# Fused attention and mixer: PSUM as one tile of eight banks, with one exponential and one normalising instruction for two heads

## The chip, the cores and the metric

The kernel runs on one core of one Trainium2 chip. The metric is the device time of one launch in microseconds. The kernel before was timed three times: median 333.76 us, from 333.57 to 334.19. One more execution was taken by the hardware profiler; its span, from the first to the last instruction on the core, is 330.8 us.

## The reference

Causal attention with 16 beacon keys in front, followed by a token mixer of rank 32 and a two-layer perceptron, both with a residual:

```python
B, H, S, Nb, D = 8, 8, 576, 16, 64          # batch, heads, tokens, beacons, head width
k_all = concat(beacon_k, k); v_all = concat(beacon_v, v)      # 592 keys
scores = q @ k_all^T / sqrt(D), causal behind the beacons
a = exp(scores - max); a /= a.sum() + 1e-9
x = (a @ v_all), heads side by side          # B x 576 x 512
h = x^T @ U @ V                              # U 576x32, V 32x576: over the tokens
u = x + h^T
out = u + relu(u @ w_ch1) @ w_ch2            # 512 -> 2048 -> 512
```

## The kernel before

**Work.** A pair is two heads of one batch; there are 32, four to a batch. The keys of a pair (592, in five chunks of 128) stand on the partitions, the queries along the free axis, so that the scores come out transposed and their exponentials can be the stationary operand of the next product. Scores go into PSUM banks (512 f32 words on each of 128 partitions) in four groups `g`, packed so that no masked block is computed: 496, 464, 496 and 208 columns a head. For each group and each head there is one bank `sps`, one exponential on ScalarE (ACT) into an SBUF tile `expt` of that head, and VectorE (DVE) zeroes the diagonal blocks with a minimum against a mask (`mask_head`, L349, one instruction a head). The weighting (`av_unit`, L424) multiplies a head's exponentials by its values with a column of ones beside them: 15 matmuls into one bank `po` of 5 x 65 words, whose 65th words are the sums. DVE takes their reciprocals (L436, 128x5) and multiplies (L437, 128x5x64) into the batch's `xb`.

`visit` inside `score_units` (L354) issues scores and exponentials of pairs 0 to 7, two groups at a time; `by_head` sets the order of its four exponentials (head 0's two first, or group by group). The outer `visit` (L396) does this for later pairs, with up to four units at a time, where a unit is one group of one pair or two short groups (208 and 208) in one bank.

The mixer of a batch (`mix_units`) ends in `most` (L486): four matmuls `ups` (L490), one for each 128 columns of the model, each on 32 rows of the array and into a bank of its own, drained on DVE by `settle` (L477). The perceptron takes 512 tokens at a time: first layer `gps` (L675) with a relu on ACT (L683) or DVE (L681), or by Strassen's seven products in `qpsA`, `qpsD`, `qpsF` (L701), which DVE adds to kept parts (L723) before a relu (L728); second layer in products `mpsA` to `mpsF` (L829, L909), which DVE adds to `kept` or `ob` tiles (L849). These steps wait in a list, `fill(n)` takes n of them.

**Order.** Every engine's order is written out by hand: the whole runs under a manual schedule, where each engine executes its instructions in the order in which Python issued them. `play` reads lines of short words (`e` scores, `a` and `b` head 0's and head 1's weighting, `m` masks, `f` one step of the list), and `long_slot` arranges the later pairs. A pair's two weightings are not neighbours: steps of the list are put between them.

**Banks.** There are eight PSUM banks. `pst` (L107) hands them out strictly in the order in which Python returned them by `emptying` (L114): first in, first out. It is called when the instructions are issued, so which bank a matmul writes is fixed in the program. The framework lets the first matmul into a bank wait for the last reader of what it held before. A bank is returned right behind its reader in program order, not when that reader has run.

```python
emptied = list(range(8))
...
b = emptied.pop(0)
t = psum.tile(shape, dtype, tag=f"bank{b}", name=name)
...
emptied.append(bank_of.pop(id(t))[0])
```

Of the kernel before, what the change touches and what calls it, by code (L numbers as in the profile page):

```python
# [18 lines left out]
P = 128  # L19
# [11 lines left out]
def kernel(  # L31
# [13 lines left out]
    nc = tc.nc  # L45
    B, H, S, D = q.shape
# [56 lines left out]

    emptied = list(range(8))
    bank_of = {}

    def pst(shape, dtype, name):  # L107

        b = emptied.pop(0)
        t = psum.tile(shape, dtype, tag=f"bank{b}", name=name)  # L110
        bank_of[id(t)] = (b, t)
        return t

    def emptying(t):  # L114
        emptied.append(bank_of.pop(id(t))[0])

# [29 lines left out]
    def clear_gaps(ex):  # L146
        for g in range(1, 4):
            nc.vector.memset(ex[:, AT[g] + gw[g] : AT[3] if g == 1 else blk[(3 if g == 3 else 4, 4)] + P], 0.0)

# [23 lines left out]
    NE = 4  # L173
    expts = [const.tile([P, EW], F16, name=f"expt{i}", tag=f"expt{i}") for i in range(NE)]
    flat = w2.rearrange("p (i a) c -> p i (a c)", i=NE)
    lent = [flat[:, i, 0:EW] for i in range(NE)]
    kTs = [const.tile([P, NH2, NC * P], F16, name=f"kT{i}", tag=f"kT{i}") for i in range(2)]
# [166 lines left out]
    def score_units(c, qT, kT, ex, early=False):  # L344

        def mask_head(i):
            e = ex[i][:, 0 : 3 * SLOT]
# [5 lines left out]
        def visit(gs, idle=0, by_head=True, between=None):  # L353
            turn = [(g, i) for i in range(2) for g in gs] if by_head else [(g, i) for g in gs for i in range(2)]  # L354
            ps = {(g, i): pst([P, 512], F32, name=f"sps{i}") for g, i in turn}
            keep_warm(ps[gs[0], 0], idle)
            if early:
                for g in gs:
                    for i in range(2):
                        for ch, qa, w, o in groups[g]:  # L360
                            if ch in (g, 4):
                                n = nq[ch]
                                nc.tensor.matmul(
                                    ps[g, i][:, ds(o, n)], identb, negmask[:, min(ch, 1), 0:n],
                                    start=ch == g, stop=False, skip_group_check=True,
                                )
            for g in gs:
                for ch, qa, w, o in groups[g]:
                    for i in range(2):
                        hp = slice(D * i, D * i + D)  # L370
                        nc.tensor.matmul(  # L371
                            ps[g, i][:, ds(o, w)], kT(hp, c, ch), qT[hp, c, ds(qa, w)],
                            start=not early, stop=True, skip_group_check=early,
                        )

            def exps(g, i):
                nc.scalar.activation(  # L377
                    out=ex[i][:, ds(AT[g], gw[g])], in_=ps[g, i][:, 0 : gw[g]], func=AF.Exp, scale=scale
                )

            for n, (g, i) in enumerate(turn):
                if between and n == len(gs):
                    between()
                exps(g, i)
                emptying(ps[g, i])

        def masks():
            for i in () if early else range(2):
                mask_head(i)

        return [
            lambda idle=0, between=None, gs=[0, 1]: visit(gs, idle, between=between),
            lambda gs=[2, 3], by_head=True: visit(gs, 0, by_head), masks, mask_head,
        ]

    def visit(parts):  # L396

        at = {p: (p % NH2, qTs[p // NH2], keys_of(p // NH2, kTs[p // NH2 % 2]), expts_of(p)) for p, _ in parts}
        both = {(p, g) for p, g in parts if g == 3 and (p + 1, 3) in parts}
        units = [[(p, g, 0), (p + 1, g, gw[g])] if (p, g) in both else [(p, g, 0)]  # L400
                 for p, g in parts if (p - 1, g) not in both]
        ps = {}
        for unit in units:
            banks = [pst([P, 512], F32, name=f"sps{i}") for i in range(2)]
            for p, g, at0 in unit:
                c, qT, kT, _ = at[p]
                for ch, qa, w, o in groups[g]:
                    for i in range(2):
                        hp = slice(D * i, D * i + D)
                        nc.tensor.matmul(  # L410
                            banks[i][:, ds(at0 + o, w)], kT(hp, c, ch), qT[hp, c, ds(qa, w)],
                            start=True, stop=True, skip_group_check=len(unit) > 1,
                        )
            ps[unit[0]] = banks
        for unit in units:
            for i in range(2):
                bank = ps[unit[0]][i]
                for p, g, at0 in unit:
                    nc.scalar.activation(  # L419
                        out=at[p][3][i][:, ds(AT[g], gw[g])], in_=bank[:, ds(at0, gw[g])], func=AF.Exp, scale=scale  # L420
                    )
                emptying(bank)

    def av_unit(b, h, ex, vs, xb):  # L424
        po = pst([P, NT, E], F32, name="po")
        for j in range(NT):
            for c in range(j + 1):
# [5 lines left out]
                    stop=(c == j),  # L433
                )
        r = rec[:, b * H + h, :, :]
        nc.vector.reciprocal(out=r, in_=po[:, :, D : D + 1])  # L436
        nc.vector.tensor_tensor(  # L437
            out=xb[:, :, ds(h * D, D)], in0=po[:, :, 0:D], in1=r.broadcast_to([P, NT, D]), op=ALU.mult
        )
        emptying(po)  # L440

    def x_into(xb, ups, cc, js, a, first):
# [778 lines left out]
    def expts_of(p):  # L1221
        return [(lent if p in (2, 3) else expts)[(2 * p + i) % NE] for i in range(2)]

# [7 lines left out]
    def av_of(p):  # L1231
        b, c = divmod(p, NH2)
        if c == 0:
            assert not coming or b < DT0
            xbs[b] = xbp.tile([P, NT, DM], F16, name="xb", tag="xb")
        return [
            lambda i=i: av_unit(b, 2 * c + i, expts_of(p)[i], vss[b % 2], xbs[b]) for i in range(2)
        ]
# [4 lines left out]
    avs = {}  # L1243
    ON_PE = (0, 1, 4)
    ACT_KEYS = (8, 10, 11, 12, 14, 15)

# [102 lines left out]
    with tc.manual_schedule(engines={ENG.PE, ENG.Activation, ENG.DVE, ENG.SP, ENG.Pool}):  # L1349
# [18 lines left out]
        cast = small_loads()  # L1368
        sc[1]([3, 2], False)
        sc = scores_of(1)  # L1370
# [26 lines left out]
        t2[1]()  # L1397
        sc[1]([3, 2], False)
        t2[0]()
        t3[1]()  # L1400
        later[0][0]()
        t3[0]()
        later[0][1]([3, 2], False)
        av[0]()
# [265 lines left out]
```

## Time and profile before

| | |
|---|---|
| time, median of 3 | 333.76 us (333.57 to 334.19) |
| span of the profiled execution | 330.8 us, at a mean granted TensorE clock of 0.998 |
| time that lies around the span, by the median | 3.0 us |
| TensorE (PE) | 323.5 us busy, 98% of the span, 3670 matmuls |
| VectorE (DVE) | 262.7 us, 79%, 606 instructions |
| ScalarE (ACT) | 196.6 us, 59%, 430 instructions |
| GpSimd (POOL) | 167.1 us, 51% |
| exponentials | L377 48 and L419 192 in the two costliest groups, 20.4 and 82.0 us |
| normalising | L436 64 times, 186 ns in the mean; L437 64 times, 491 ns |

In the rows of the trace a line shows the start in microseconds from the span's beginning, the busy time, engine, line and operation, output and inputs by the program's names, shapes, and the number of equal instructions in a row; in brackets stands the engine's idle time before, with what ended it. In rows that group instructions, the numbers behind the bar are the group's busy time, the mean of one in ns, and the idle time ahead of the group with its releasers. A row of stretches shows for each engine its busy time in that stretch with its number of instructions, in the order PE, weight loads, DVE, ACT, POOL, and then the granted clock, the DMA share and the rate. Spans of neighbouring instructions of one engine overlap a little, because an end includes the tail of writing.

### The profile page before, as it was taken

The numbers are of one execution on the slowest core, as the hardware profiler recorded it, in microseconds if no ns is written. First come the engines' busy times: TensorE is split into PE (matmuls) and PEld (weight loads), VectorE is DVE, ScalarE is ACT, GpSimd is POOL, SyncE is SP. The second block draws the span as 40 slices with busy tenths as digits, with TensorE's granted clock in tenths as the row PEclk, the third lists the DMA queues.
The fourth block names the chain that finished last, engine by engine and source line by source line (L and its number), as shares of the span: only waits on it lengthen the run. The fifth ranks groups of instructions, "written<-read, shape, count | busy, mean of one in ns | idle before, by whom it ended". The sixth has DMA issues, their size and how long they took to land.

```text
span 330.8 us, 9298 instructions
## 1 busy us (share of the span) xinstructions
PE 323.5 (98%) x3670; PEld 228.9 (69%) x3670; DVE 262.7 (79%) x606; ACT 196.6 (59%) x430; POOL 167.1 (51%) x263
## 2 busy tenths in 40 slices
PE   8899999999999999999999999999999999999994
PEld 3565555555578656876588888765787888788783
DVE  6675888668998668786878777877788898798993
ACT  5967962689972677348844695379636613713710
POOL 8897734568238960689048923950284036030030
PEclk9999999999999999999999999999999999999999
DMA  7999999999999996999999999995014512305004
GB/s 159 142 168 156 173 190 202 193 193 156 97 129 164 196 153 98 96 183 138 131 166 165 138 139 152 98 216 80 12 65 117 74 44 98 65 8 168 19 4 131
DMA packets 150562, 41.99 MB, mean 127 GB/s; under 512 B 131313, under 2 KB 149937, under 8 KB 150513
## 3 DMA queue, kind: packets, MB, share of 16 engines
q0 software_dynamic: 87568, 18.18, 73.2%
q1 hardware_dynamic: 62144, 22.41, 38.1%
q10 hardware_dynamic: 800, 0.75, 0.7%
q8 instruction: 30, 0.49, 0.7%
q14 instruction: 20, 0.16, 0.2%
HBM read 37.45 MB, written 9.44 MB: 142 GB/s over the span
## 4 chain that ended last, share of the span: by engine, by line
PE 94%; ACT 3%; DVE 1%; issue 0%
PE gps L675 21%; PE po L428 9%; PE mpsA L909 9%; PE qpsA L701 6%; PE mpsD L829 6%; PE sps L410 6%; PE cps L1053 4%; PE gps L1027 4%; PE mpsE L829 3%; PE mpsC L829 3%; PE mpsB L829 3%; PE qpsD L701 3%; ACT expt L377 2%; PE mpsF L829 2%; PE mpsD L909 2%; PE tps L299 2%
## 5 line engine op out<-in xcount | busy, mean ns | idle before, releaser
L577 POOL TENSOR_TENSOR ob<-ob,ut 128x128 f32<-128x128 f32 x104 | 50.0, 510 | 121.2 <-DVE ob L849 59.4
L419 ACT ACTIVATE expt<-sps 128x496 f16<-128x496 f32 (+2 forms) x192 | 82.0, 542 | 41.8 <-PE sps L410 41.8
L675 PE MATMUL gps<-uT,w 128*128 128x512 f16 (+1 forms) x368 | 78.1, 351 | 0.0
L829 PEld LDWEIGHTS <-gT 128*128 128x128 f16 x576 | 54.2, 98 | 8.8 <-issue 2.6
L675 PEld LDWEIGHTS <-w 128*128 128x128 f16 x368 | 33.2, 98 | 25.6 <-issue 1.3
L653 DVE TENSOR_TENSOR gT<-gT 128x1024 f16<-128x1024 f16 (+3 forms) x87 | 47.0, 561 | 0.9
L239 POOL DMA_DIRECT2D vs<-in_v_dram x50 | 40.0, 810 | 14.9 <-DMA w<-in_moe_w_ch_dram 11.2
L683 ACT ACTIVATE gT<-gps 128x512 f16<-128x512 f32 x63 | 37.5, 619 | 16.1 <-PE gps L675 11.9
L428 PEld LDWEIGHTS <-expt 128*128 128x128 f16 x900 | 33.9, 98 | 7.9 <-issue 1.5
L428 PE MATMUL po<-vs,expt 128*128 128x65 f16 x900 | 36.4, 194 | 0.2
L909 PEld LDWEIGHTS <-gT 128*128 128x128 f16 x336 | 31.2, 98 | 4.0
L437 DVE TENSOR_TENSOR xb<-po,rec 128x320 f16<-128x320 f32 x64 | 31.4, 491 | 2.2
L349 DVE TENSOR_TENSOR expt<-expt,bigmask 128x768 f16<-128x768 f16 x54 | 30.3, 600 | 0.4 <-ACT expt L419 0.2
L720 ACT ACTIVATE kept<-qpsA 128x512 f32<-128x512 f32 x18 | 10.9, 603 | 24.1 <-PE qpsA L701 13.2
L436 DVE RECIPROCAL rec<-po 128x5 f32<-128x5 f32 x64 | 11.9, 186 | 13.6 <-PE po L428 13.2
L410 PE MATMUL sps<-qT,kT 64*128 64x80 f16 (+4 forms) x288 | 22.6, 281 | 0.0
L377 ACT ACTIVATE expt<-sps 128x496 f16<-128x496 f32 (+2 forms) x48 | 20.4, 569 | 0.6 <-PE sps L371 0.6
L909 PE MATMUL mpsA<-w,gT 128*128 128x256 f16 x160 | 19.1, 273 | 0.0
L410 PEld LDWEIGHTS <-kT 64*128 64x128 f16 x288 | 10.2, 94 | 12.8 <-issue 8.3
L681 DVE TENSOR_SCALAR gT<-gps 128x512 f16<-128x512 f32 x17 | 11.7, 689 | 8.9 <-PE gps L675 8.7
L1126 POOL DMA_DIRECT2D st<-in_k_dram x20 | 16.9, 859 | 1.2 <-DVE pr L294 0.9
L1126 POOL DMA_DIRECT2D st<-in_q_dram x20 | 16.9, 872 | 0.7 <-DVE rec L436 0.7
(159 smaller groups left out, 541.4 us busy)
## 6 DMA issues: line engine op xcount, KB each, us to landing
out_dram<-ob SPq DMA_DIRECT2D x33, 256.0 KB, 3.5
vs<-in_v_dram POOLq DMA_DIRECT2D x18, 128.0 KB, 6.7
w<-in_moe_w_ch_dram POOLq DMA_DIRECT2D x4, 512.0 KB, 6.2
w<-in_moe_w_ch_dram POOLq DMA_DIRECT2D x2, 1024.0 KB, 12.7
st<-in_k_dram POOLq DMA_DIRECT2D x12, 128.0 KB, 6.6
st<-in_q_dram POOLq DMA_DIRECT2D x12, 128.0 KB, 8.6
st<-in_k_dram POOLq DMA_DIRECT2D x4, 288.0 KB, 12.0
st<-in_q_dram POOLq DMA_DIRECT2D x4, 288.0 KB, 12.6
```

Source lines behind the costliest of these rows:

```text
L239: nc.gpsimd.dma_start(out=dst[a : a + nq[j], j, :, :], in_=src[hs, ds(q0[j], nq[j]), :].rearrange("h p d -> p h d"))
L410: nc.tensor.matmul(banks[i][:, ds(at0 + o, w)], kT(hp, c, ch), qT[hp, c, ds(qa, w)], start=True, stop=True, skip_group_check=len(unit) > 1,)
L419: nc.scalar.activation(out=at[p][3][i][:, ds(AT[g], gw[g])], in_=bank[:, ds(at0, gw[g])], func=AF.Exp, scale=scale)
L428: nc.tensor.matmul(po[:, j, :], ex[0 : nk[c], ds(blk[(c, j)], P)], vs[0 : nk[c], ds(c * H * E + h * E, E)], start=(c == 0), stop=(c == j),)
L437: nc.vector.tensor_tensor(out=xb[:, :, ds(h * D, D)], in0=po[:, :, 0:D], in1=r.broadcast_to([P, NT, D]), op=ALU.mult)
L577: nc.gpsimd.tensor_tensor(out=o[:, i, ds(c, w)], in0=x[:, i, ds(c, w)], in1=y[:, i, ds(c, w)], op=op)
L653: nc.vector.tensor_tensor(out=o[:, ds(d0, n)], in0=x[:, ds(d0, n)], in1=y[:, ds(d0, n)], op=op)
L675: nc.tensor.matmul(g[:, ds(o, w)], w1[:, cc, ts(dc, P)], uT[:, cc, ds(at, w)], start=(cc == 0 and o == 0), stop=(cc == NCC - 1), skip_grou ...
L683: nc.scalar.activation(out=cell["g"][:, dc, :], in_=g, func=AF.Relu)
L829: nc.tensor.matmul(ps, a()[:, d, ds(P * i, P)], bm[:, d, ds(c0, w)], start=fresh and d == 0 and i == 0, stop=d == HF - 1, skip_group_check ...
L909: nc.tensor.matmul(ps, a()[:, d, ds(P * i, P)], bm[:, d, ds(c0, w)], start=fresh and d == 0, stop=d == HF - 1, skip_group_check=True,)
L1126: coming.append(lambda d=dst, s=src, a=m[j] - nq[j], n=m[j], j=j: nc.gpsimd.dma_start(out=d[a:n, j, :, :], in_=s[:, ds(q0[j], nq[j]), :].r ...
```

## The change

PSUM becomes one tile, `whole`, of eight banks. Four things follow in the code.

- **One exponential for both heads.** The scores of head 0 and head 1 of a group are put into neighbouring banks, the `expt` tiles hold both heads side by side, and one activation reads 2 x 496 (or 464, 208) words. ACT issues 32 instead of 64 exponentials at L377 and 96 instead of 192 at L419 in the program. The order of `by_head` falls away. The minimum with the mask stays one instruction a head.
- **One normalising for both heads.** All pairs but 0, 1, 2, 3 and 7 (`APART`) use `av_both`: two neighbouring banks are taken when head 0's weighting starts, and behind head 1's stand one reciprocal of 10 and one multiplication of 2 x 5 x 64. Both banks are returned there. 27 pairs do so.
- **How single banks are chosen.** `pst` looks at the three that were returned first (`SOON`) and takes the one without which most neighbouring pairs are left among the free; among equals the oldest.
- **How pairs are chosen.** `pst2s(n)` looks at all ways to take n pairs of neighbours from the free banks and takes the one whose later members were returned earliest; they are handed out in that order.

PE's matmuls and weight loads, their shapes and their order stay the same, instruction by instruction. On DVE 54 fewer instructions stand in the program for the normalising (27 reciprocals and 27 multiplications), and 12 fewer that clear gaps in `expt`.

```diff
@@ pst @@
     emptied = list(range(8))
+    SOON = 3
+    whole = psum.tile([P, 8, 512], F32, name="whole", tag="whole")
     def pst(shape, dtype, name):
-        b = emptied.pop(0)
-        t = psum.tile(shape, dtype, tag=f"bank{b}", name=name)
+        b = max(emptied[:SOON], key=lambda x: (twos(y for y in emptied if y != x), -emptied.index(x)))
+        emptied.remove(b)
+        t = whole[0 : shape[0], b, :]
...
+    def twos(free):
+        free, n = sorted(free), 0
+        while free:
+            b = free.pop(0)
+            if b + 1 in free:
+                free.remove(b + 1)
+                n += 1
+        return n
+    def pst2s(n):
...
+        def late(bs):
+            return sum(2.0 ** max(emptied.index(b), emptied.index(b + 1)) for b in bs)
+        got = sorted(min(sets(n, 0), key=late), key=lambda b: late([b]))
...
     def emptying(t):
-        emptied.append(bank_of.pop(id(t))[0])
+        b, _, *more = bank_of.pop(id(t))
+        emptied.extend([b, *more])
@@ visit, first pairs @@
-            turn = [(g, i) for i in range(2) for g in gs] if by_head else [(g, i) for g in gs for i in range(2)]
-            ps = {(g, i): pst([P, 512], F32, name=f"sps{i}") for g, i in turn}
+            ps = dict(zip(gs, pst2s(len(gs))))
...
+            for n, g in enumerate(gs):
+                if between and n == 1:
+                    between()
                 nc.scalar.activation(
-                    out=ex[i][:, ds(AT[g], gw[g])], in_=ps[g, i][:, 0 : gw[g]], func=AF.Exp, scale=scale
+                    out=ex[:, :, ds(AT[g], gw[g])], in_=ps[g][:, :, 0 : gw[g]], func=AF.Exp, scale=scale
...
+                emptying(ps[g])
@@ visit, later pairs @@
+        free = pst2s(len(units))
         for unit in units:
-            banks = [pst([P, 512], F32, name=f"sps{i}") for i in range(2)]
+            banks = ps[unit[0]] = free.pop(0)
...
-            for i in range(2):
-                bank = ps[unit[0]][i]
...
-                        out=at[p][3][i][:, ds(AT[g], gw[g])], in_=bank[:, ds(at0, gw[g])], func=AF.Exp, scale=scale
+                    out=at[p][3][:, :, ds(AT[g], gw[g])], in_=banks[:, :, ds(at0, gw[g])], func=AF.Exp, scale=scale
@@ weighting @@
+    def av_both(b, h, ex, vs, xb):
+        cell = {}
+        def head(i):
+            if i == 0:
+                cell["t"] = pst2()
+            po = cell["t"][:, :, 0 : NT * E].rearrange("p h (j e) -> p h j e", e=E)
+            weigh(po[:, i], ex[:, i, :], vs, h + i)
+            if i == 0:
+                return
+            r = rec[:, ds(b * H + h, 2), :, :]
+            nc.vector.reciprocal(out=r, in_=po[:, :, :, D : D + 1])
+            nc.vector.tensor_tensor(
+                out=xb[:, :, ds(h * D, 2 * D)].rearrange("p j (h d) -> p h j d", d=D), in0=po[:, :, :, 0:D],
+                in1=r.broadcast_to([P, 2, NT, D]), op=ALU.mult,
+            )
+            emptying(cell["t"])
+        return [lambda i=i: head(i) for i in range(2)]
...
+    APART = (0, 1, 2, 3, 7)
```

How the instructions stand shows at three places. The first is PE, at the mixer's four `ups` of one batch, near 170.7 us of the trace before: the four follow the last matmul into `mpsB`. `qts` is the batch's input to the mixer in transposed form, `Vsb` the matrix V; in brackets stand the engines whose progress a matmul waits for. Before:

```order
L829 MATMUL mpsB<-wt,gT 128x256
L490 LDWEIGHTS qts
L490 MATMUL ups<-Vsb,qts 128x496 [waits Activation_49]
L490 LDWEIGHTS qts
L490 MATMUL ups<-Vsb,qts 128x496 [waits Activation_49]
L490 LDWEIGHTS qts
L490 MATMUL ups<-Vsb,qts 128x496 [waits Activation_49]
L490 LDWEIGHTS qts
L490 MATMUL ups<-Vsb,qts 128x496 [waits Activation_49]
L428 LDWEIGHTS expt_108 [waits DVE_49]
L428 MATMUL po<-vs_112,expt_108 128x65 [waits Activation_49]
```

With the change:

```order
L896 MATMUL whole<-wt,gT 128x256
L557 LDWEIGHTS qts
L557 MATMUL whole<-Vsb,qts 128x496
L557 LDWEIGHTS qts
L557 MATMUL whole<-Vsb,qts 128x496 [waits Activation_49]
L557 LDWEIGHTS qts
L557 MATMUL whole<-Vsb,qts 128x496
L557 LDWEIGHTS qts
L557 MATMUL whole<-Vsb,qts 128x496 [waits DVE_49]
L470 LDWEIGHTS expt_107
L470 MATMUL whole<-vs_111,expt_107 128x65
```

Nothing moved; the first and the third of the four no longer wait for an instruction of ACT, and the fourth, which writes the bank that `mpsB` held, waits for one of DVE, the addition of `mpsB` to `kept`.

The second place is DVE near 153 to 157 us of the trace before: `rec` and `xb` belong to one pair, the two sums with `kept` (L723, after: L790) and the relu behind them (L728, after: L795) to the perceptron. Before, head 0's normalising stands between the two sums and head 1's behind the relu:

```order
L723 TENSOR_TENSOR gT<-qpsD,kept 128x2x256 [waits Activation_49]
L436 RECIPROCAL rec<-po 128x5 [waits PE_49]
L437 TENSOR_TENSOR xb<-po,rec 128x5x64 [waits DVE_49]
L723 TENSOR_TENSOR gT<-qpsD,kept 128x2x256 [waits PE_49]
L728 TENSOR_SCALAR gT<-gT 128x2x2x256 [waits DVE_49]
L436 RECIPROCAL rec<-po 128x5 [waits PE_49]
L437 TENSOR_TENSOR xb<-po,rec 128x5x64 [waits DVE_49]
L681 TENSOR_SCALAR gT<-gps 128x512 [waits PE_49]
```

With the change:

```order
L790 TENSOR_TENSOR gT<-whole,kept 128x2x256 [waits Activation_49]
L790 TENSOR_TENSOR gT<-whole,kept 128x2x256 [waits PE_49]
L795 TENSOR_SCALAR gT<-gT 128x2x2x256 [waits DVE_49]
L500 RECIPROCAL rec<-whole 128x10 [waits PE_49]
L501 TENSOR_TENSOR xb<-whole,rec 128x2x5x64 [waits DVE_49]
L748 TENSOR_SCALAR gT<-whole 128x512 [waits PE_49,Activation_49]
```

Head 0's two instructions are gone from between the two sums, and one reciprocal and one multiplication for both heads stand where head 1's were.

The third place is ACT at its first exponentials, in the first 20 us. Before, each head has its own, and `expt_105` and `expt_106` are the two heads' tiles:

```order
L377 ACTIVATE expt_105<-sps_230 128x464 [waits PE_49]
L377 ACTIVATE expt_105<-sps_231 128x496 [waits PE_49]
L377 ACTIVATE expt_106<-sps_232 128x464
L377 ACTIVATE expt_106<-sps_233 128x496 [waits PE_49]
L377 ACTIVATE expt_105<-sps_282 128x208 [waits PE_49]
L377 ACTIVATE expt_106<-sps_283 128x208 [waits PE_49]
L377 ACTIVATE expt_105<-sps_284 128x496 [waits PE_49]
L377 ACTIVATE expt_106<-sps_285 128x496 [waits PE_49]
```

With the change, where `expt_106` holds both heads:

```order
L426 ACTIVATE expt_106<-whole 128x2x464 [waits PE_49]
L426 ACTIVATE expt_106<-whole 128x2x496 [waits DVE_49,PE_49]
L426 ACTIVATE expt_106<-whole 128x2x208 [waits DVE_49,PE_49]
L426 ACTIVATE expt_106<-whole 128x2x496 [waits PE_49]
L426 ACTIVATE expt_107<-whole 128x2x496 [waits PE_49]
```

Eight instructions have become four, each over two banks; a fifth row shows the next pair's first.

More of the change, by code (lines that the diff above doesn't have):

```diff
@@ L173 @@
     NE = 4
-    expts = [const.tile([P, EW], F16, name=f"expt{i}", tag=f"expt{i}") for i in range(NE)]
+    expts = [const.tile([P, 2, EW], F16, name=f"expt{i}", tag=f"expt{i}") for i in range(NE // 2)]
     flat = w2.rearrange("p (i a) c -> p i (a c)", i=NE)
-    lent = [flat[:, i, 0:EW] for i in range(NE)]
+    lent = [flat[:, 2 * i : 2 * i + 2, 0:EW] for i in range(NE // 2)]
     kTs = [const.tile([P, NH2, NC * P], F16, name=f"kT{i}", tag=f"kT{i}") for i in range(2)]
@@ L1221, in expts_of @@
     def expts_of(p):
-        return [(lent if p in (2, 3) else expts)[(2 * p + i) % NE] for i in range(2)]
+        return (lent if p in (2, 3) else expts)[p % 2]
     def scores_of(p):
@@ L1235, in av_of @@
             xbs[b] = xbp.tile([P, NT, DM], F16, name="xb", tag="xb")
+        if p not in APART:
+            return av_both(b, 2 * c, expts_of(p), vss[b % 2], xbs[b])
         return [
-            lambda i=i: av_unit(b, 2 * c + i, expts_of(p)[i], vss[b % 2], xbs[b]) for i in range(2)
+            lambda i=i: av_unit(b, 2 * c + i, expts_of(p)[:, i, :], vss[b % 2], xbs[b]) for i in range(2)
         ]
@@ L1402 @@
         t3[0]()
-        later[0][1]([3, 2], False)
+        later[0][1]([3, 2])
         av[0]()
```

67 lines of the change are left out of this document (44 added, 23 removed).

## The prediction

> **What bounds the kernel now.** I began with the page: busy shares, slices, granted clock, chain.
>
> ```profile
> span 330.8 us, 9298 instructions
> PE 323.5 (98%) x3670; PEld 228.9 (69%) x3670; DVE 262.7 (79%) x606; ACT 196.6 (59%) x430; POOL 167.1 (51%) x263
> ...
> PE   8899999999999999999999999999999999999994
> ...
> PEclk9999999999999999999999999999999999999999
> ...
> PE 94%; ACT 3%; DVE 1%; issue 0%
> ```
>
> TensorE (PE) is busy in 98% of the span and carries 94% of the chain of waits that ended last, at full clock. Only the first two slices, 16.5 us, are below nine tenths. DVE at 79% and ACT at 59% are not the bound. So a shorter instruction on DVE or ACT gains nothing by itself after the first slices, and every new wait of PE is paid in full, since PE has no slack in which to catch up. The question is therefore not what the merged instructions save, but whether each PSUM bank still comes free before PE wants it.
>
> The change leaves PE's instructions and their order as they are. What it alters is the bank each one writes, hence the instruction that has to have emptied that bank. So I took each PE instruction that opens a bank, looked up who last emptied its new bank, and set that instruction's end in the trace against PE's start. In before none of these comes out negative. With the new banks some forty do, in four kinds.
>
> **The prices.** From the groups by shape, and one row that shows what a hand-over costs:
>
> ```profile
> L419 ACT ACTIVATE expt<-sps 128x496 f16<-128x496 f32 x96 | 51.2, 604 | 10.7 <-PE sps L410 10.7
> ...
> L419 ACT ACTIVATE expt<-sps 128x208 f16<-128x208 f32 x48 | 13.2, 371 | 30.6 <-PE sps L410 30.6
> ```
> ```profile
> L437 DVE TENSOR_TENSOR xb<-po,rec 128x320 f16<-128x320 f32 x64 | 31.4, 491 | 2.2
> L849 DVE TENSOR_TENSOR kept<-mpsB,kept 128x512 f32<-128x512 f32 x6 | 4.1, 689 | 1.0 <-PE mpsB L829 1.0
> ```
> ```profile
> 156.16 0.49 DVE L437 TENSOR_TENSOR xb<-po,rec 128x320 f16<-128x320 f32 x1
> ```
> ```profile
> 156.70 0.11 PEld L675 LDWEIGHTS <-w 128*128 128x128 f16 x2 [0.47 <-DVE xb L437]
> ```
>
> Normalising one head (320 elements a partition) is 0.49 us, a 512-element DVE instruction on PSUM 0.69, so an element costs (689 − 491)/192 = 1.03 ns, and a merged one of 640 an estimated 0.49 + 0.33 = 0.82. No row shows one with four dimensions: its bounds are 0.49 (no longer than one head's) and 0.98 (two run one after the other); 0.82 lies on the line through both rows. DVE saves about 0.16 + a reciprocal per pair, some 8 us in 27 pairs, behind other work. From an end on DVE (156.16 + 0.49 = 156.65) to the start on PE (156.70) is 0.05. A wait thus adds: the emptier's end + 0.05 − PE's start in the trace.
>
> **First kind: the four ups matmuls.** They start together right behind mpsB. The rule that keeps neighbours together passes the older banks by and gives the fourth the bank that mpsB has just left, which L849 must still add to kept. In before they take the four oldest.
>
> ```profile
> 101.48 0.39 PE L490 MATMUL ups<-Vsb,qts 32*128 32x496 f16 x4
> ...
> 136.33 0.39 PE L490 MATMUL ups<-Vsb,qts 32*128 32x496 f16 x4
> ...
> 170.67 0.39 PE L490 MATMUL ups<-Vsb,qts 32*128 32x496 f16 x4
> ...
> 205.06 0.39 PE L490 MATMUL ups<-Vsb,qts 32*128 32x496 f16 x4
> ```
> ```profile
> 101.27 0.69 DVE L849 TENSOR_TENSOR kept<-mpsB,kept 128x512 f32<-128x512 f32 x1 [0.16 <-PE mpsB L829]
> ...
> 136.44 0.69 DVE L849 TENSOR_TENSOR kept<-mpsB,kept 128x512 f32<-128x512 f32 x1 [0.16 <-PE mpsB L829]
> ...
> 170.85 0.69 DVE L849 TENSOR_TENSOR kept<-mpsB,kept 128x512 f32<-128x512 f32 x1 [0.23 <-PE mpsB L829]
> ...
> 205.24 0.69 DVE L849 TENSOR_TENSOR kept<-mpsB,kept 128x512 f32<-128x512 f32 x1 [0.23 <-PE mpsB L829]
> ```
>
> 101.27 + 0.69 + 0.05 − 101.48 = 0.53, and so 0.85, 0.92, 0.92: together 3.2 us. DVE was idle and waiting for PE at each L849, so nothing that DVE saves makes these ends earlier. Behind the waiting matmul stand head 0's weighting (L428) and all of PE. Two later stages take older banks and pay nothing.
>
> **Second kind: a bank of a normalised pair.** Both heads' banks are now held until the merged instruction ends, and the next taker stands soon after. Each pair of rows is the old head 1's normalising and the PE row that opens a bank of that pair in the new order.
>
> ```profile
> 121.17 0.49 DVE L437 TENSOR_TENSOR xb<-po,rec 128x320 f16<-128x320 f32 x1
> ...
> 149.31 0.49 DVE L437 TENSOR_TENSOR xb<-po,rec 128x320 f16<-128x320 f32 x1
> ...
> 154.63 0.69 DVE L723 TENSOR_TENSOR gT<-qpsD,kept 128x512 f16<-128x512 f32 x1 [0.16 <-PE qpsD L701]
> ...
> 182.06 0.68 DVE L723 TENSOR_TENSOR gT<-qpsF,kept 128x512 f16<-128x512 f32 x1
> ...
> 183.65 0.49 DVE L437 TENSOR_TENSOR xb<-po,rec 128x320 f16<-128x320 f32 x1
> ...
> 190.49 0.49 DVE L437 TENSOR_TENSOR xb<-po,rec 128x320 f16<-128x320 f32 x1
> ...
> 224.65 0.49 DVE L437 TENSOR_TENSOR xb<-po,rec 128x320 f16<-128x320 f32 x1
> ```
> ```profile
> 121.23 0.34 PE L410 MATMUL sps<-qT,kT 64*128 64x208 f16 x4
> ...
> 149.64 0.27 PE L701 MATMUL qpsD<-st,lw 128*128 128x256 f16 x1
> ...
> 155.69 0.60 PE L675 MATMUL gps<-uT,w 128*128 128x512 f16 x2
> ...
> 181.16 0.60 PE L701 MATMUL qpsF<-uT,w 128*128 128x256 f16 x4
> ...
> 183.24 0.37 PE L410 MATMUL sps<-qT,kT 64*128 64x496 f16 x2
> ...
> 190.08 0.39 PE L675 MATMUL gps<-uT,w 128*128 128x256 f16 x2
> ...
> 224.41 0.60 PE L675 MATMUL gps<-uT,w 128*128 128x512 f16 x2
> ```
>
> At 0.82 + 0.05 after the start on DVE: 121.17 + 0.87 − 121.23 = 0.81; 156.16 + 0.87 − 155.69 = 1.34; 190.49 and 224.65 in the same way 1.28 and 1.11. At these last three, L723 ahead of the normalising waits for PE's qpsD (154.63), so DVE cannot come earlier. At 149 and 183 it can: the old head 0's normalising stood ahead of L723 and is gone. But L723 needs qpsF, which ends at 181.16 + 0.60 = 181.76, +0.05; it began at 182.06, so 0.25 is gained and no more. That leaves 149.31 + 0.87 − 149.64 − 0.26 = 0.28 and 183.65 + 0.87 − 183.24 − 0.26 = 1.02. Sum of the six: 5.8 us.
>
> **Third kind: one relu behind the merged instruction.**
>
> ```profile
> 218.00 0.49 DVE L437 TENSOR_TENSOR xb<-po,rec 128x320 f16<-128x320 f32 x1
> 218.41 0.68 DVE L681 TENSOR_SCALAR gT<-gps 128x512 f16<-128x512 f32 x1
> ```
> ```profile
> 218.37 0.49 PE L701 MATMUL qpsD<-st,lw 128*128 128x256 f16 x3
> ```
>
> qpsD now takes the bank that L681 empties. L681 moves 0.33 later with the merged instruction and 0.26 earlier as above: 218.48 + 0.68 + 0.05 − 218.37 = 0.8 us.
>
> **Fourth kind: scores, and the beginning.** A bank pair comes free only when the exponential of both heads is done, where head 0's bank came free half-way. ACT is nearly full only here:
>
> ```profile
> 7.00:20.40 13.40, 11.94 (x235) 8.17 (x232) 9.72 (x27) 13.22 (x32) 12.41 (x22) 1.00 1.57 147
> ```
> ```profile
> 44.73 0.59 ACT L377 ACTIVATE expt<-sps 128x464 f16<-128x464 f32 x1
> ```
> ```profile
> 44.66 0.38 PE L428 MATMUL po<-vs,expt 128*128 128x65 f16 x7
> ```
>
> 32 instructions in 13.22 us are 0.413 each. The four shapes of a visit (464, 496, 208, 496) have 416 elements in the mean, at (604 − 371)/288 = 0.81 ns each 0.34 us; 0.07 is left as the price of an instruction, and 16 fewer save at most 1.1 us. Against it stand waits for the second half; the largest is po at 44.66, whose new bank is emptied at 44.73 + 0.59 = 45.32: 0.6 to 0.7 us. Summing those up to 48 us I take +1.5, between −1.1 (all hidden, ACT's gain whole) and +2.5. Later, about ten of 0.03 to 0.2 us remain, taken at 0.6 (0 to 1.2).
>
> Here a rule speaks against the change. The Trainium skill, "Perfetto Trace Analysis", section "Optimizing Scalar/DVE Operations", says that larger operations help when their engine is saturated, and that when ScalarE or DVE are not saturated but cause bubbles elsewhere, "breaking up instructions may allow work to be completed sooner". By it the change would be a loss wherever ACT and DVE have room; the trace agrees in that DVE stands at 79% and ACT at 59% of the span, with ACT full only before 20 us. The same section puts the fixed part at about 125 ns for DVE on PSUM; by that the merged normalising would be an estimated 0.86 us and the sum about 0.3 longer.
>
> **The sum.** 3.2 + 5.8 + 0.8 + 1.5 + 0.6 = 11.9 us on the profiled span of 330.8: 342.7. Around the span lie 333.76 − 330.8 = 3.0 us of the median, so about 345.7, 3.6% over the median 333.76. Low end: merged at 0.49 (six waits and the relu 0.33 shorter, the smallest not below zero: 3.9 and 0.5), 3.2, beginning −1.1, nothing later: 6.5, so 340.3. High end: merged at 0.98 (seven by 0.16 longer): 3.2 + 6.8 + 1.0 + 2.5 + 1.2 = 14.7, so 348.5.
>
> **Rivals.**
>
> *Faster.* The beginning gains its 1.1 us and the waits are covered, because PE's order slips a little at each and the next emptier is then on time: 332.7. For it speaks that after one wait the others are relatively earlier; against it, that the emptiers at most sites themselves follow PE (the bracketed releasers above), so they slip with it. It would decide if DVE and ACT were late at these places for reasons other than PE. 0.06.
>
> *DVE runs ahead.* The 8 us that DVE saves put it far enough ahead that kinds two and three vanish: 3.2 + 1.5 + 0.6 = 5.3, so 339.1. Against it, L723 waits for PE directly ahead of three of the seven. 0.07.
>
> *The clock drops.* Short waits of PE might cost clock too.
>
> ```profile
> 1.19 3.59 PE L274 MATMUL idle<-w 128*128 128x512 f16 x8 [1.19 <-DVE ones L159]
> ```
>
> Eight 512-wide matmuls after an idle start take 3.59 us, 0.45 each; two of the warm stretch (224.41) take 0.60 with the tail. If each of eleven waits brought such a stretch back, at about half speed, that is 11 × 1.8 = 20 us: about 366. Against it, the trace has a wait of 1.19 at its start but later slices at full clock throughout. The Trainium skill, "TensorE: Matmul & The Clock Gate", section "A second HAM failure mode: psum-queue depth-cycling", describes just this, short idle times between groups that let the clock swing; section "What's actually happening" puts the idle window at about 3.4 us. My longest wait is 1.34, and no run here shows a drop after one. 0.03.
>
> *No effect.* The banks come out otherwise than I followed them, and nothing on PE's path changes: 333.8. 0.03.
>
> **Chances.** Forecast 0.81, faster 0.06, DVE ahead 0.07, clock 0.03, no effect 0.03. What a measurement of this kernel can tell from no change is about 0.2%. Faster by more 0.06, within 0.03, slower 0.91. The range runs from 338.5, which takes in the case of DVE ahead, to 349.5, a little over the high end; about 0.12 of the cases and the forecast's own error lie outside.
>
> **What would show it.** In the profile after, PE waits should appear, with releaser kept L849 at the four ups (0.5 to 0.9 each), with xb at five or six places (0.3 to 1.3) and gT L748 once near 230 us; PE's share of the chain should fall by about 3% of the span and DVE's rise by as much. The merged normalising's mean should be about 0.82 us, the merged 496-wide exponential's 1.0 to 1.15, PE's busy time unchanged, the clock full. I am wrong if those matmuls start without a wait, if the merged DVE instruction is far from 0.82, or if the first 48 us come out shorter by over a microsecond.

## The result and the profile after

The changed kernel takes 345.34 us (median of 5, 344.94 to 346.57) against 333.76 (median of 5, 333.15 to 334.19). The medians are 11.6 us apart, a ratio of 1.0347; the ratio on record is 1.0369, with a 95% interval of 1.0348 to 1.0389, and how the two come apart is not shown. The forecast was 345.7, its span 342.7. The first fence is the page of the changed kernel: span, busy times, the shares of the chain.

```profile
span 343.2 us, 9128 instructions
PE 326.8 (95%) x3670; PEld 230.0 (67%) x3670; DVE 257.3 (75%) x540; ACT 190.4 (55%) x302; POOL 167.4 (49%) x263
...
PEclk9999999999999999999999999999999999999999
...
PE 83%; DVE 6%; ACT 1%; issue 0%; ACTq 0%; DVEq 0%
```

DVE is 5.4 us and ACT 6.2 us less busy than before, and the profiled execution is 12.4 us longer (343.2 against 330.8). PE issues the same 3670 matmuls; what is new is that it waits. The next fence is the view of PE's waits after the change: what waited, for what, the sum in us, the number of waits, the longest.

```profile
PE whole L742 <- DVE xb L501: 3.2, 3, 1.1
PE whole L455 <- DVE xb L501: 1.8, 2, 1.1
PE whole L557 <- DVE kept L916: 1.5, 3, 0.5
...
PE whole L768 <- DVE gT L748: 0.7, 1, 0.7
...
PE whole L470 <- ACT expt L426: 0.5, 1, 0.5
PE whole L410 <- ACT expt L426: 0.5, 1, 0.5
PE whole L768 <- DVE xb L501: 0.4, 1, 0.4
```

In before this view has four rows with 2.3 us in all, none of them later than 20 us:

```profile
PE idle L274 <- DVE ones L159: 1.2, 1, 1.2
PE sps L371 <- DVE qT L332: 0.5, 1, 0.5
PE po L428 <- DVE w L349: 0.4, 1, 0.4
PE sps L363 <- ACT expt L377: 0.2, 1, 0.2
```

A wait listed here is shorter than what it costs, since PE counts as busy while the tail of the matmul before is still running. For the cost I matched PE's matmuls one by one between the two traces, which is possible because they are the same in the same order, and read by how much the distance between the starts grows at each place:

| place in before, us | predicted | measured step |
|---|---|---|
| up to 48 (scores) | 1.5 | 1.96 |
| 48 to 101 and other small ones | 0.6 | 0.7 |
| ups at 101.5, 136.3, 170.7, 205.1 | 0.53, 0.85, 0.92, 0.92 | 0.52, 0.84, 0.91, 0.91 |
| pair's bank at 121.2 | 0.81 | 0.85 |
| 149.6 | 0.28 | 0.58 |
| 155.7 | 1.34 | 1.14 |
| 183.2 | 1.02 | 1.31 |
| 190.1 | 1.28 | 1.13 |
| 224.4 | 1.11 | 1.13 |
| relu's bank at 218.4 | 0.8 | 0.85 |
| sum | 11.9 | 12.8, of which 0.16 is given back at 156.7 and 0.09 between 190 and 205; 12.6 at the last matmul |

Each kind can be read in the trace of the changed kernel. The ups: three start, the fourth 0.92 later, when the addition to kept has ended (177.29 + 0.69 = 177.98).

```profile
177.12 0.39 PE L557 MATMUL whole<-Vsb,qts 32*128 32x496 f16 x3
178.04 0.36 PE L557 MATMUL whole<-Vsb,qts 32*128 32x496 f16 x1 [0.54 <-DVE kept L916]
```
```profile
177.29 0.69 DVE L916 TENSOR_TENSOR kept<-whole,kept 128x512 f32<-128x512 f32 x1 [2.12 <-PE whole L896]
```

A pair's bank, and the relu behind the merged instruction (191.02 + 0.82 = 191.84, PE at 191.90; 229.09 + 0.68 = 229.77, PE at 229.82):

```profile
191.02 0.82 DVE L501 TENSOR_TENSOR xb<-whole,rec 128x640 f16<-128x640 f32 x1
...
229.09 0.68 DVE L748 TENSOR_SCALAR gT<-whole 128x512 f16<-128x512 f32 x1
```
```profile
191.90 0.38 PE L455 MATMUL whole<-qT,kT 64*128 64x496 f16 x2 [1.15 <-DVE xb L501]
...
229.82 0.38 PE L768 MATMUL whole<-st,lw 128*128 128x256 f16 x2 [0.69 <-DVE gT L748]
```

The groups by shape give the merged instructions' own durations:

```profile
L501 DVE TENSOR_TENSOR xb<-whole,rec 128x640 f16<-128x640 f32 x27 | 22.3, 824 | 0.9
```
```profile
L462 ACT ACTIVATE expt<-whole 128x992 f16<-128x992 f32 x48 | 47.7, 1000 | 11.5 <-PE whole L455 11.5
```

824 ns is the 0.82 of the estimate, and 1000 ns lies at the low end of the 1.0 to 1.15 given for the exponential. The 0.86 us worked out from the fixed part in the Trainium skill, "Perfetto Trace Analysis", section "Optimizing Scalar/DVE Operations", was 0.04 too long. The same passage calls that part an engine-busy time and puts the profiled latency at about twice it; by that the estimate would have been 0.73, 0.09 too short. The measured duration decides.

### The profile page after: what moved, and what is told of

It reads as the page before. It is cut to its first block, busy times and chain, and to the rows that moved or that the text cites. A ratio compares the mean times of both kernels' runs of the same rounds, so it can differ in the third digit from the quotient of the medians.

```text
span 343.2 us, 9128 instructions
## 1 busy us (share of the span) xinstructions
PE 326.8 (95%) x3670; PEld 230.0 (67%) x3670; DVE 257.3 (75%) x540; ACT 190.4 (55%) x302; POOL 167.4 (49%) x263
## 4 chain that ended last, share of the span: by engine, by line
PE 83%; DVE 6%; ACT 1%; issue 0%; ACTq 0%; DVEq 0%
PE whole L742 20%; PE whole L896 19%; PE whole L976 10%; PE whole L768 10%; PE whole L470 7%; PE whole L455 5%; PE whole L1120 4%; PE whole L1094 3%; DVE xb L501 2%; PE whole L347 1%; DVE gT L790 1%; PE whole L418 1%; DVE gT L795 1%; DVE kept L916 1%; PE whole L532 1%; PE whole L557 1%
## 5 line engine op out<-in xcount | busy, mean ns | idle before, releaser
L462 ACT ACTIVATE expt<-whole 128x992 f16<-128x992 f32 (+2 forms) x96 | 76.1, 868 | 45.7 <-PE whole L455 38.9
L742 PE MATMUL whole<-uT,w 128*128 128x512 f16 (+1 forms) x368 | 77.8, 351 | 3.2 <-DVE xb L501 3.2
L750 ACT ACTIVATE gT<-whole 128x512 f16<-128x512 f32 x63 | 37.5, 602 | 26.0 <-PE whole L742 26.0
L896 PE MATMUL whole<-wt,gT 128*128 128x256 f16 x384 | 46.8, 273 | 0.0
L470 PEld LDWEIGHTS <-expt 128*128 128x128 f16 x900 | 33.9, 98 | 11.6 <-issue 4.9
L470 PE MATMUL whole<-vs,expt 128*128 128x65 f16 x900 | 36.6, 194 | 0.9 <-ACT expt L426 0.5
L455 PE MATMUL whole<-qT,kT 64*128 64x80 f16 (+4 forms) x288 | 23.6, 281 | 1.8 <-DVE xb L501 1.8
L976 PE MATMUL whole<-w,gT 128*128 128x256 f16 (+1 forms) x200 | 23.0, 268 | 0.0
L896 PE MATMUL whole<-w,gT 128*128 128x256 f16 x192 | 23.0, 273 | 0.0
L501 DVE TENSOR_TENSOR xb<-whole,rec 128x640 f16<-128x640 f32 x27 | 22.3, 824 | 0.9
L790 DVE TENSOR_TENSOR gT<-whole,kept 128x512 f16<-128x512 f32 x18 | 12.4, 689 | 14.0 <-ACT kept L787 10.6
L916 DVE TENSOR_TENSOR ob<-whole,kept 128x512 f32<-128x512 f32 x22 | 15.1, 684 | 8.5 <-PE whole L896 8.4
L748 DVE TENSOR_SCALAR gT<-whole 128x512 f16<-128x512 f32 x17 | 11.7, 686 | 11.3 <-PE whole L742 11.2
## 6 DMA issues: line engine op xcount, KB each, us to landing
w<-in_moe_w_ch_dram POOLq DMA_DIRECT2D x2, 1024.0 KB, 12.8
st<-in_q_dram POOLq DMA_DIRECT2D x4, 288.0 KB, 12.6
```

What stands on the lines that cost most here:

```text
L455: nc.tensor.matmul(banks[:, i, ds(at0 + o, w)], kT(hp, c, ch), qT[hp, c, ds(qa, w)], start=True, stop=True, skip_group_check=len(unit) > 1,)
L462: nc.scalar.activation(out=at[p][3][:, :, ds(AT[g], gw[g])], in_=banks[:, :, ds(at0, gw[g])], func=AF.Exp, scale=scale)
L470: nc.tensor.matmul(po[:, j, :], ex[0 : nk[c], ds(blk[(c, j)], P)], vs[0 : nk[c], ds(c * H * E + h * E, E)], start=(c == 0), stop=(c == j),)
L742: nc.tensor.matmul(g[:, ds(o, w)], w1[:, cc, ts(dc, P)], uT[:, cc, ds(at, w)], start=(cc == 0 and o == 0), stop=(cc == NCC - 1), skip_grou ...
L750: nc.scalar.activation(out=cell["g"][:, dc, :], in_=g, func=AF.Relu)
L896: nc.tensor.matmul(ps, a()[:, d, ds(P * i, P)], bm[:, d, ds(c0, w)], start=fresh and d == 0 and i == 0, stop=d == HF - 1, skip_group_check ...
```

## The experiments

The theory to be tested: the whole of the loss is PE waiting for banks. It has three parts, the rule that chooses banks, the holding of two banks until one instruction has read both, and the scores of the first 48 us. The rivals: that the single tile makes instructions wait more than they must, or that merged instructions are slow in themselves. Times of the runs below are compared with the kernel before on their own chip: 333.07 us for the run with one tile and the three of the beginning, 333.2 for the four others.

### One tile, nothing else

The kernel before, with banks as slices of one tile, still first in, first out.

```diff
+    whole = psum.tile([P, 8, 512], F32, name="whole", tag="whole")
...
         b = emptied.pop(0)
-        t = psum.tile(shape, dtype, tag=f"bank{b}", name=name)
+        t = whole[0 : shape[0], b, :]
...
```

> The kernel before with PSUM as one tile of eight banks and nothing else: every bank is handed out first in, first out, nothing is merged, each wait falls on the same instruction as before. Theory: same time as before, 333.2 on this kind of run. Rival (one tile makes instructions wait for more than their own bank): slower by a microsecond or more.

333.0 us, ratio 0.9994 (0.9982 to 1.0007). The single tile costs nothing that can be measured, by the interval 0.2 us at most.

### The newest bank for the fourth ups, nothing merged

```diff
-        b = emptied.pop(0)
+        b = emptied.pop(-1 if newest else 0)
...
-            ups = [pst([P, QM], F32, name="ups") for _ in range(NCC)]
+            ups = [pst([P, QM], F32, name="ups", newest=i == NCC - 1) for i in range(NCC)]
```

> The kernel before, nothing merged, first in first out, but for one choice: the fourth of the mixer's ups matmuls takes the bank that was returned last. Theory (PE pays for every bank that is emptied after it wants it): in the trace of before the new waits are 1.26 us at 101.5 (an exponential that ends at 102.70), 0.84 at 136.3, 0.91 at 170.7, 205.1 and 239.2, 0.84 at 270.4: together 5.7, so 339.4 us. Rival (the change is slow because merged instructions or the single tile are slow, and the choice of banks is harmless): 333.8.

338.1 us, ratio 1.0146 (1.0128 to 1.0164), 4.9 us over before. Matched with before, PE falls behind by 1.26, 0.84, 0.91, 0.91, 0.91 and 0.84 us at the six places and nowhere else to speak of: 5.5 at the last matmul of the profiled execution. In the view of PE's waits:

```profile
PE ups L490 <- DVE kept L849: 2.5, 5, 0.5
...
PE ups L490 <- ACT expt L419: 0.9, 1, 0.9
```

So six badly chosen banks, with every instruction as before, cost 1.5% of the time. The size came out 0.2 us (last matmul) to 0.8 us (medians) below the 5.7 of the expectation.

### The same banks, normalising one head at a time

```diff
             weigh(po[:, i], ex[:, i, :], vs, h + i)
+            r = rec[:, b * H + h + i, :, :]
+            nc.vector.reciprocal(out=r, in_=po[:, i, :, D : D + 1])
+            nc.vector.tensor_tensor(
+                out=xb[:, :, ds((h + i) * D, D)], in0=po[:, i, :, 0:D], in1=r.broadcast_to([P, NT, D]), op=ALU.mult
+            )
             if i == 0:
                 return
-            r = rec[:, ds(b * H + h, 2), :, :]
...
             emptying(cell["t"])
```

> The changed kernel with the same banks for everything, but the two heads normalised by two reciprocals and two multiplications, each right behind its head's weighting. Theory: head 0's bank is now read earlier, and the waits of PE for it vanish (at 121, 149, 156, 190 and 224 us of before, measured 0.84, 0.56, 1.13, 1.14, 1.14, together 4.8); at 183 and 218 the bank is head 1's or stands behind its normalising, and about 0.4 is gained; the ups' waits stay. So 345.3 - 5.2 = 340.1 us, with DVE busier by about 8 us. Rival (a merged instruction costs by its own length, DVE's time being what counts): DVE longer by 8 us, time not below 345.

339.78 us, ratio 1.0193 (1.0175 to 1.0212): 6.6 us over before, 6.3 expected, where the changed kernel is 11.6 over. The steps at 121, 149, 156, 190 and 224 us are gone; at 183 it is 0.95 in place of 1.31, at 218 0.94, and the ups' stay (0.52, 0.84, 0.84, 0.84). The page shows that DVE is busier for it, while the kernel is faster:

```profile
span 338.8 us, 9185 instructions
PE 326.4 (96%) x3670; PEld 229.7 (68%) x3670; DVE 264.5 (78%) x594; ACT 190.0 (56%) x302; POOL 167.1 (49%) x263
```

264.5 against 257.3 us of DVE, and 5.0 us gained by the medians (11.6 less 6.6), 5.4 at the last matmul of the two traces, 5.9 by the ratios (3.69% less 1.93%). What mattered is when head 0's bank has been read, not what DVE has to do. This is the case of the sentence in the Trainium skill, "Perfetto Trace Analysis", section "Optimizing Scalar/DVE Operations", on breaking up instructions that cause bubbles on another engine, and these two runs bear it out.

### All merged, with a searched list of banks

The changed kernel, in which each request takes its bank from a written list. The list was searched so that the sum of waits is smallest, with the starts and ends of before's trace.

```diff
+    TABLE = [
...
         b = max(emptied[:SOON], key=lambda x: (twos(y for y in emptied if y != x), -emptied.index(x)))
+        if turn_of[0] < len(TABLE):
+            b = TABLE[turn_of[0]]
+            turn_of[0] += 1
...
+            got = TABLE[turn_of[0] : turn_of[0] + n]
...
```

> The changed kernel's instructions, exponentials and normalisings merged, with a written list of banks in place of the rule: the list was searched so that PE waits least by the times in before's trace. Theory: what the rule costs goes, what the holding of two banks costs stays; by before's times waits of 0.5 at 101.5, 0.2 to 0.5 at 121.5, 0.55 at 149.6, 184.0 and 218.4, 0.78 at 155.7, 190.1 and 224.4 are left, 4.9 in all, and up to 0.6 in the first 48 us: 339.2 us. Rival A (the rule alone is to blame, eight banks are enough): 334. Rival B (merged instructions are slow by themselves): 345.

338.92 us, ratio 1.019 (1.0156 to 1.0224); 5.7 over before, 5.4 expected. The rule thus costs 5.9 us by the medians, about 1.8% (3.69 − 1.90), and what this list could not remove is left. The steps are 0.52 at 101.5, 0.59 at 121.5, 0.51, 0.51 and 0.50 at 149.6, 184.0 and 218.4, and 0.78 three times at 155.7, 190.1 and 224.4. At the last six the list could do no better than a bank that an exponential was still reading:

```profile
PE whole L766 <- ACT expt L486: 2.1, 3, 0.7
...
PE whole L792 <- ACT expt L486: 1.0, 3, 0.3
```

With a pair's two banks held until both heads are normalised, eight banks are not enough at these places, as far as my search could find; it was not exhaustive.

### Exponentials merged, normalising one head at a time, searched list

```diff
+    TABLE = [
...
-    APART = (0, 1, 2, 3, 7)
+    APART = tuple(range(32))
```

> Exponentials merged for all pairs, normalising a head at a time, with a list of banks searched in the same way. Theory: by before's times no wait is left behind 45 us; in the first 45 us some of 0.1 to 0.4 remain, against which ACT's 16 fewer instructions stand: 333.8 to 334.8, so the merged exponential costs nothing and gains nothing where PE is the bound. Rival (the merged exponential is itself late for PE, since two banks come free at once): 336 or more.

334.73 us (333.91 to 337.06), ratio 1.0046 (1.0029 to 1.0064). It is 4.2 us under the run with both merged, on the same chip: that is the price of holding two banks, 4.9 by the waits in the expectation of that run. The rule's 5.9, this 4.2 and the 1.5 that are left make up the 11.6. Behind 48 us PE falls behind by only 0.2 us, so the merged exponentials of pairs 8 to 31 cost nothing. The 1.5 us over before lie in the first 48 us: with the exponentials of those pairs left one for each head they are gone (next section). Its profiled execution was the slowest of the five and shows something else there, told in the last section.

### The beginning taken apart

Three kernels with normalising one head at a time and lists of their own, in which the exponentials of some of the first eight pairs are one for each head, in the order of before: pairs 0 to 7, then 4 to 7 only, then 0 to 3 only.

```diff
+    SINGLE = tuple(range(8))
...
+            for n, (g, i) in enumerate(turn if apart else [(g, 0) for g in gs]):
```

> Exponentials merged for pairs 8 to 31 only, one for each head in the first 48 us, normalising a head at a time, written list of banks. Theory: by before's times no bank is wanted before it is empty, and PE is the bound, so 96 exponentials fewer on ACT change nothing: 333.0 to 333.5, same as before. Rival 1 (merged exponentials are late by themselves): 334.5 or more. Rival 2 (ACT's time counts after all): below 332.5.

> As the run with exponentials merged for pairs 8 to 31, and those of pairs 0 to 3 merged too (the first 20 us, where ACT is full); pairs 4 to 7 one for each head. Theory: ACT saves up to 1.1 us there, but both banks of a pair come free together, and copies on DVE then stand later: between -0.5 and +0.6 against before, 332.7 to 333.8. Rival (the first 20 us explain the whole of the 1.5 us that merging all exponentials cost): 334.5.

> As the run with exponentials merged for pairs 8 to 31, and those of pairs 4 to 7 merged too (20 to 48 us); pairs 0 to 3 one for each head. Theory: waits of 0.16 to 0.38 at 33, 39, 44 us remain by before's times, and the mask of the pair at 47 us stands behind the merged exponential: +0.6 to +1.1, 333.8 to 334.3. Rival (this stretch costs nothing, all of it comes from the first 20 us): 333.2.

| merged | us, median of 12 | ratio to before, interval |
|---|---|---|
| pairs 8 to 31 | 332.49 | 0.9985 (0.9972 to 0.9997) |
| and pairs 0 to 3 | 333.97 | 1.0022 (1.0010 to 1.0035) |
| and pairs 4 to 7 | 333.10 | 1.0005 (0.9986 to 1.0023) |

With 96 exponentials fewer on ACT and no bank wanted too early, the time is that of before to within 0.15%; by the interval it is a little faster, and it is the fastest of all versions, though only 0.5 to 0.6 us under the one-tile version and before. It lies below the 333.0 to 333.5 expected, and just within the second rival's "below 332.5". The trace speaks against that rival: PE's lead is only 0.23 us at the last matmul. Of this, 0.12 is there at 20 us, where no exponential is merged yet; it appears at 18.65 us of before, where PE waited for DVE's mask. The rest comes in one step at 156.7. Which part of the edit did that was not tried.

Merging the first four pairs costs 1.5 us against not merging them, more than I gave it (332.7 to 333.8). ACT is relieved there, 15.62 us busy in the first 20 against 16.15, but PE waits elsewhere. PE's waits with the first four pairs merged, and then with none of the first eight:

```profile
PE whole L448 <- DVE qT L405: 1.2, 2, 0.7
PE whole L440 <- DVE kT L410: 0.7, 1, 0.7
```
```profile
PE whole L449 <- DVE qT L406: 0.6, 1, 0.6
```

The second wait for qT and that for kT are new. The one for kT is a wait for a bank: the matmul reads only `negmask` and `identb`, and in this list the bank that it opens is emptied by DVE's copy of kT, where it is an exponential with none of the first eight merged:

```profile
11.61 0.25 PE L440 MATMUL whole<-negmask,identb 128*128 128x128 bf16 x2 [0.69 <-DVE kT L410]
```
```profile
11.21 0.25 PE L441 MATMUL whole<-negmask,identb 128*128 128x128 bf16 x2 [0.23 <-ACT expt L458]
```

That copy of kT is no later than in the other run (11.40 against 11.37). PE is 0.40 late from here, and so are its transposes of the next pair's queries and keys (12.20 against 11.80) and DVE's copy of qT behind them (12.76 against 12.29). This explains less than half of the 1.5 us: against the run with none merged PE is 0.6 us late at 20 us and no more at the last matmul. The spans differ by 1.4, and the other 0.8 lies behind the last matmul (5.5 us against 4.7); why is open.

Pairs 4 to 7 cost 0.6 us against the first row, at the low end of what I gave them, but against before, by which the expectation gave 333.8 to 334.3, they cost nothing: 333.10 is where its rival stood, and the intervals of the two rows overlap. In the traces PE is 0.45 us later at 48 us than in the first row's run. Of the waits expected at 33, 39 and 44 us only 0.18 at 39.7 appeared, and was given back at once; 0.35 at 47.9 us, behind the mask, did appear.

## Why the prediction was right

**The number.** 345.7 against 345.34 is in part luck, for two misses offset each other. The sum of waits was 0.7 us too small, 11.9 against 12.6 at the last matmul. And the 3.0 us taken as lying around the span were too many: in every execution of every run with both figures on record, before and after alike, the time is 1.65 to 1.84 us longer than the span. So the profiled execution of before, whose span of 330.8 was the base of the sum, was some 1.2 us quicker than the median, and that of the changed kernel 0.4; this is why the spans are 12.4 apart and the medians 11.6.

**The bound.** PE had no slack and every wait was paid, while 5 to 6 us less on DVE and ACT bought nothing. The pair of runs with one and with two normalisings on the same banks shows it most plainly: DVE up by 7 us, time down by 5.0 to 5.9. One reading was incomplete: not only the first two slices of PE are below nine tenths but also the last one, at four, where before spends 4.6 us behind its last matmul.

**First kind, 3.2 us:** measured 3.18. The run that makes only this choice, in the old kernel, shows that the choice alone does it.

**Second kind, 5.8:** measured 6.14, 5.98 with what is given back at 156.7. That is closer than its terms are. Two terms were too small, at 149 and 183 us (0.28 and 1.02, measured 0.58 and 1.31). The step that failed is the 0.26 us by which DVE was to come earlier: I took only the end of qpsF as its limit. L723, now L790, also waits for ACT's copy of qpsA, which ended hardly earlier:

```profile
181.36 0.60 ACT L720 ACTIVATE kept<-qpsA 128x512 f32<-128x512 f32 x1 [0.24 <-PE qpsA L701]
```
```profile
189.39 0.69 DVE L790 TENSOR_TENSOR gT<-whole,kept 128x512 f16<-128x512 f32 x1 [0.53 <-ACT kept L787]
```

181.36 + 0.60 = 181.96 against the start at 182.06 in before: 0.05 was to be had once a hand-over is counted. The terms at 156 and 190 were 0.2 and 0.15 too large. I had held that DVE cannot come earlier there, because L723 waits for PE. It did wait, but the relu between it and the normalising (L728, now L795) was shorter, as it was at the place of the third kind. Before, and then after:

```profile
155.36 0.67 DVE L728 TENSOR_SCALAR gT<-gT 128x1024 f16<-128x1024 f16 x1
189.75 0.61 DVE L728 TENSOR_SCALAR gT<-gT 128x1024 f16<-128x1024 f16 x1
217.16 0.72 DVE L728 TENSOR_SCALAR gT<-gT 128x512 f16<-128x512 f16 x1
```
```profile
160.82 0.43 DVE L795 TENSOR_SCALAR gT<-gT 128x1024 f16<-128x1024 f16 x1
198.41 0.43 DVE L795 TENSOR_SCALAR gT<-gT 128x1024 f16<-128x1024 f16 x1
227.76 0.43 DVE L795 TENSOR_SCALAR gT<-gT 128x512 f16<-128x512 f16 x1
```

The sum also left out that the merged reciprocal is longer than one head's: the multiplication starts 0.25 behind it (161.16 to 161.41), where it was 0.21 (155.95 to 156.16). With both, 1.34 − 0.24 + 0.04 = 1.14 and 1.28 − 0.18 + 0.04 = 1.14, against 1.14 and 1.13 measured. Why the same relu takes 0.43 at one time and 0.6 to 0.7 at another is not shown.

**Third kind, 0.8:** 0.85. The same 0.26 failed here too, and the relu L795, 0.29 shorter than L728 had been (the third row above), made up for it: again a right size in part by luck. The relu L748 began at 229.09, 0.74 after the merged instruction, as reckoned, and PE 0.05 after its end.

**Fourth kind, 1.5 and 0.6:** measured 1.96 and 0.7. The runs by stretch show that ACT's gain of 1.1 us in the first 20 us, which I had set against the waits, was saved on ACT only in part (0.5 to 0.7 us) and did not reach PE.

**Rivals.** DVE did not run ahead: the waits for xb and for the relu are in the trace. The clock did not drop in the changed kernel (0.997 to 1.000 in the mean of each of its five executions). "Faster" and "no effect" are out.

**What would show it.** Releasers and sizes came nearly as listed; of the four ups the view lists three, at 0.5 each. Two items did not come: PE's busy time is not unchanged but 3.3 us more, with the same instructions (the tails of matmuls that no longer overlap the next one are the likely reason; not tested), and PE's share of the chain fell by 11 points, not 3, while DVE's rose by 5; the rest is in no engine that the line lists, and I can't say where.

## What to carry over

When a kernel's bound engine has no slack, list for each of its waits the end of the releaser and the start of the waiter, and redo that list with the new owners of each buffer; here it gave the loss to within a microsecond, while the busy times of DVE and ACT fell. Merging two instructions that empty two buffers holds the first buffer for as long as the second takes, and the rule that keeps buffers in neighbouring pairs handed out the newest one at the ups. In this kernel, where the emptying engines are not the bound, both cost more than the saved instructions bring; where such an engine is the bound was not tried. Merge where the buffers are not wanted soon after, and check it place by place.

## What the runs showed of the hardware

I had not expected a drop of the clock from short waits, and in one execution there was one. In the profiled execution of the kernel with all exponentials merged and normalising one head at a time (337.06 us, the slowest of its five), a load came late, DVE's cast waited for it, and PE waited 1.49 us; with other waits of 0.7 us PE was busy 1.51 and 1.65 us in two stretches of 3 us. The clock then stood at about half from 15 to 22 us:

```profile
8.11 0.59 DVE L365 CAST pr<-stkq 96x768 f16<-96x768 f32 x1 [1.57 <-DMA stkq<-in_q_dram]
```
```profile
8.75 0.43 PE L372 MATMUL whole<-ident,pr 96*128 96x96 f16 x6 [1.49 <-DVE pr L365]
```
```profile
6.00:9.00 3.00, 1.51 (x18) 0.77 (x17) 1.07 (x2) 2.29 (x4) 2.78 (x5) 1.00 1.24 179
...
12.00:15.00 3.00, 1.65 (x40) 1.22 (x40) 1.74 (x4) 2.74 (x4) 3.00 (x5) 1.00 1.46 144
15.00:18.00 3.00, 2.71 (x32) 1.31 (x31) 1.34 (x3) 2.52 (x4) 2.72 (x8) 0.53 1.30 128
18.00:21.00 3.00, 3.00 (x45) 2.13 (x43) 1.37 (x4) 1.70 (x3) 2.94 (x7) 0.50 1.22 186
```

The columns are the stretch, its length, busy time and instructions of PE, weight loads, DVE, ACT and POOL, then the clock, the DMA share and the rate. No wait there was longer than 1.5 us. In the changed kernel, single waits of up to 1.15 us between full stretches left the clock at full, and so did the stretch from 12 to 15 us with PE busy 2.01 us of 3. So the third rival, which I gave 0.03, may have its place where waits gather, as in the start of a kernel. The Trainium skill, "TensorE: Matmul & The Clock Gate", section "What's actually happening", puts the idle window behind such a drop at about 3.4 us; here the longest single wait was less than half of that. It is one execution, and what decides between the two was not tried. Two more have a mean clock as low: the slowest of the kernel with all merged and a searched list (340.81 us at 0.991, the other three 338.39 to 339.10 at 0.998 or more), and the slowest with the first four pairs merged (334.54 at 0.988, no slower than the next at 334.53). No trace of them was kept, so where their clock fell is not known.
